# Spreading a per-batch softmax chain over the units of a spectral filter, its subtraction of one on another engine

## The chip, the cores and the metric

The kernel runs on one core of one Trainium2 chip. The metric is the time of one execution on the device in microseconds, the median of several runs.

## The reference

Three stages follow each other on `x` of 8 batches, 3072 tokens, 256 channels, all in float32.

```python
X = np.fft.rfft(x, axis=1)                       # per batch, along the tokens
y = np.fft.irfft(X * (filt_r + 1j * filt_i), n=3072, axis=1)
x = y.reshape(8 * 3072, 256)

logits = x @ phi                                 # 32 slots
d = np.exp(logits - logits.max(0, keepdims=True))     # softmax over ALL tokens
slot_input = (d / (d.sum(0, keepdims=True) + 1e-9)).T @ x
...                                              # 8 experts: relu(s @ w1[e]) @ w2[e]
c = np.exp(logits - logits.max(1, keepdims=True))     # softmax over the slots
x = (c / (c.sum(1, keepdims=True) + 1e-9)) @ slot_out

g, val = x @ w_gate, x @ w_val
out = (g / (1 + np.exp(-g)) * val) @ w_out
```

## The kernel before

`phase1` computes the filter, the logits and the first softmax; `transition` the experts; `phase2` the second softmax and the gated product. The change lies in `phase1` alone.

The FFT is two stages of matmuls. A **step** is one half (128 channels) of a batch, so there are 16 steps; a step has 6 **units**, so there are 96 units, numbered `i`, and 12 of them to a batch. One loop issues them, and since the schedule is manual, each engine's order is the order in which the Python code issues. In a unit stand, in this order:

- `s2_unit` (second stage): 8 matmuls into `X` (two PSUM buffers), which need the whole of `b`, the step's first-stage result; two products `P` and `Q` on VectorE; two sums on GpSimd into `y`.
- `tail_ops`: `tr_unit`, four transposes of the `y` of two units ago into `T` (one buffer) and a copy on ScalarE to `yt`; in every other unit `phi_pair`, the logits' matmuls into `L`, added up in `lts`. When a batch's last `lts` is there, its chain (below) is made and queued.
- `spread`: the ScalarE copies into `b` of the first-stage groups issued since.
- `aside`: one step of a side job (first the cutting of the weights from float64 to float32, `conv`, on VectorE, ScalarE and GpSimd; then `first_weights`, which reads logits back from memory).
- `pump(1)`: one step of the chain.
- `plan[u]`: which of the four first-stage groups of the **next** step (`s1_chunk`) this unit issues: a matmul group into `s` (one PSUM buffer), and its transposition on VectorE to `sg`, which `spread` copies in the next unit.
- a second `pump` in every third unit and in the last ten; a second `aside`.

The **chain** of a batch is a generator whose `yield`s cut it into steps: transposes of `lts` (L346), an inverse DFT (L356), transposes (L366) to `t4`, logits per token (L380) with their maximum `cm` on VectorE and a copy `lg` on ScalarE, an empty step, the maximum over the batch (L391), the subtraction of the maximum (L397, L400) and the exponential on ScalarE, minus one (L410; the constant part is put back at `dt`), a forward DFT (L415, `bd`, L422, `dt`, L443, `dh`), and the weighted sum of the filtered tokens (L453) into `sl`, which is stored. It runs during the next batch's units. The chains of batches 0 to 5 run in the full loop; that of batch 6 is stopped after 9 steps (`HOLD`) and finished with that of batch 7 after the loop, in an order written out by hand.

Where a chain step allocates `small()`, it takes the one PSUM buffer `c`; `lh`, `us`, `dt`, `dh` and `sl` take turns in one SBUF buffer each (tags `twa`, `twb`).

Of the kernel before, what the change touches and what calls it, by code (L numbers as in the profile page):

```python
# [17 lines left out]
NB, SEQ, D, E = 8, 3072, 256, 32  # L18
# [61 lines left out]
def spectral_softmoe_glu_kernel(  # L80
# [18 lines left out]
    pe, dve, act, pool = nc.tensor, nc.vector, nc.scalar, nc.gpsimd  # L99
# [32 lines left out]
    def phase1():  # L132
        with ExitStack() as c1:
# [30 lines left out]
            def load_x(step, k):  # L164
                b, h = divmod(step, 2)
                if b >= NB:
                    return

                if k == 0:
                    xt[step] = xp[step % 2].tile([128, 2, 16, 128], F32, tag="x", name="x")  # L170
                xr = x[b].rearrange("(p h r n) d -> r h p n d", h=2, r=2, n=16)
                for r in range(2):
                    nc.sync.dma_start(  # L173
                        out=xt[step][64 * r:64 * r + 48, k], in_=xr[r, k, :, :, h * 128:(h + 1) * 128]
                    )
# [91 lines left out]
            def tr_unit(step, u):  # L267
                b, h = divmod(step, 2)
                y = yt[b, u][:, :, :, h * 128:(h + 1) * 128]
                ps = ps_t.tile([128, 2, 2, 128], F32, tag="T", name="T")  # L270
                for i in range(2):
                    for ri in range(2):
                        pe.transpose(out=ps[:, i, ri, :], in_=y[:, i, ri, :], identity=ident)  # L273
                t = ytp.tile([128, 2, 2, 128], F32, tag="yt", name="yt")
                act.copy(t, ps)  # L275
                ytr[step, u] = t
# [24 lines left out]
            def chain(b, last):  # L301
# [3 lines left out]
                def two(late=False):  # L305

                    if late and b == NB - 2:
                        return [p.tile([128, 512], F32, tag=t, name="cl") for p, t in ((ps_t, "T"), (ps_l, "L"))]
                    if not last:
                        ps = small()  # L310
                        return [ps[:, 0:512], ps[:, 512:1024]]
                    banks[0] ^= 1
                    if not banks[0]:
                        return [ps_x.tile([128, 512], F32, tag="X", name="cl") for _ in range(2)]
                    ps = ps_s1.tile([128, 1024], F32, tag="s1", name="cl")
                    return [ps[:, 0:512], ps[:, 512:1024]]
# [18 lines left out]
                def col(t, k, n=128):  # L335

                    w = 512 // n
                    return t[k // w][:, k % w * n:(k % w + 1) * n]
# [4 lines left out]
                es2 = [slice(0, 16), slice(16, 32)]  # L343
# [10 lines left out]
                for jj in range(NJ):  # L354
                    g, k = jj % 4, jj // 4
# [16 lines left out]
                if last:  # L372
                    lg = [pq.tile([96, 16, 32], F32, tag="P", name="lg", bufs=3) for _ in es2]
                else:
                    lg = chp.tile([96, E, 32], F32, tag="lg", name="lg")
                    lg = [lg[:, es, :] for es in es2]
                cm = chp.tile([96, E], F32, tag="cm", name="cm")
                pl = two()
                for es, p in zip(es2, pl):
                    pe.matmul(out=p[0:96], lhsT=i2_sb, rhs=t4[:, es, :])  # L380
                for es, p, l in zip(es2, pl, lg):
                    dve.tensor_reduce(
                        out=cm[:, es], in_=p[0:96].rearrange("p (e n) -> p e n", n=32), axis=AX.X, op=ALU.max
                    )
                    act.copy(l, p[0:96].rearrange("p (e n) -> p e n", n=32))
                    nc.scalar.dma_start(out=lgd[b][:, es, :], in_=l)
                yield
# [10 lines left out]
                dd = chp.tile([96, E, 32], F32, tag="t4", name="dd")  # L398
# [6 lines left out]
                    )  # L405
                    act.activation(dd[:, es, :], dd[:, es, :], AF.Exp)
                if not last:
                    yield
                for es in es2:
                    (dve if last else pool).tensor_scalar_add(dd[:, es, :], dd[:, es, :], -1.0)  # L410
                yield
                bd = chp.tile([128, E, 32], F32, tag="lg", name="bd")
                pl = two()
# [6 lines left out]
                for jj in range(NJ):  # L420
                    g, k = jj % 4, jj // 4
# [28 lines left out]
                for q in range(3):  # L450
                    for ri in range(2):
                        for g in range(4):
                            pe.matmul(  # L453
                                out=ps[32 * g:32 * g + 32, 0:D],
                                lhsT=col(dh, 8 * q + 4 * ri + g, 32),
                                rhs=yt[b, 2 * q + g // 2][:, g % 2, ri, :],
                                start=(q == 0 and ri == 0),
                                stop=(q == 2 and ri == 1),
                                tile_position=(0, 32 * g),
                            )  # L460
                    if last and q:
                        rb, pss = next(com)
                    elif q == 1:
                        yield
                if b == NB - 2:
                    sl = slots[1][:, 2, :]
# [155 lines left out]
                spread()  # L622

            todo = []
            gens = []
            units = [(s, u) for s in range(2 * NB) for u in range(6)]
            plan = [[0], [1], [2], [3], [], []]

            steps = [0] * NB

            def pump(n):

                for _ in range(n):
                    while gens and steps[NB - 2] < HOLD:
                        b, g = gens[0]
                        steps[b] += 1
                        if next(g, 0) != 0:
                            break
                        gens.pop(0)

            def tail_ops(i):
                if 0 <= i - 2 < len(units):
                    tr_unit(*units[i - 2])
                if i - 4 >= 0 and i % 2 == 0 and i - 3 < len(units):
                    s, u = units[i - 4]
                    phi_pair(s, u // 2)
                    if s % 2 == 1 and u == 4:
                        gens.append((s // 2, chain(s // 2, s // 2 == NB - 1)))

            def aside():  # L650
                if next(side[0], 0) == 0 and len(side) > 1:
                    side.pop(0)

            for i, (s, u) in enumerate(units):
                if u in (0, 2):
                    load_x(s + 2, u // 2)
                s2_unit(s, u)
                tail_ops(i)
                spread()
                if i >= 4:  # L660
                    aside()
                pump(1)
                for c in plan[u]:
                    s1_chunk(s + 1, c)
                if u == 5:
                    bt.pop(s)
                pump(1 if i % 3 == 2 or i >= len(units) - 10 else 0)
                if i == 88:
                    kept(0)
                    kept(1)  # L670
                if i >= 4:
                    aside()
# [4 lines left out]
                flat_load(w1s[e], w1[e], 128)  # L677
            for i in range(len(units), len(units) + 4):
                tail_ops(i)
            (_, g6), (_, g7) = gens  # L680
            for g in (g7, g7, g7, g6, g7, g6, g7, g7, g6, g7, g6, g6):
                next(g, None)
            for _ in g7:
# [338 lines left out]
```

## Time and profile before

| | |
|---|---|
| median of 3 runs | 1586.67 us (1585.38 to 1588.87) |
| the profiled execution | 1588.74 us, of which the trace's span is 1587.0 us |
| mean granted TensorE clock | 0.977 of 2.4 GHz |
| TensorE busy (matmuls) | 1498.5 us, 94% |
| VectorE busy | 1186.1 us, 75% |
| ScalarE busy | 956.8 us, 60% |
| GpSimd busy | 257.9 us, 16%, nearly all of it in `phase1` |

The span is from the first to the last instruction. PE is TensorE's matmuls, PEld its weight loads, DVE VectorE, ACT ScalarE, POOL GpSimd. Times within the trace are in us from the span's start.

### The profile page before, as it was taken

Reading aid. Unit: us, or ns where it says so; the run is one execution under the profiler, and the core shown is the slowest. Engines: PE = TensorE matmul, PEld = TensorE weight load, DVE = VectorE, ACT = ScalarE, POOL = GpSimd, SP = SyncE. Lnnn points to the kernel's source line nnn. Section 1 sums busy time; section 2 is a strip of 40 time slices with the busy share of each in tenths; the row PEclk is TensorE's granted clock in tenths of the full one; section 3 lists DMA queues with packets and bytes.
Section 4 is the critical chain, followed back from the end, with each engine's and each line's share of the span. In section 5 each row is a group of like instructions: output and inputs, shape, how many; then the busy total and the mean of one; then the engine's idle time right before and its main releaser. Section 6 shows DMA issues by size and latency. Waiting matters only on the chain.

```text
span 1587.0 us, 26489 instructions
## 1 busy us (share of the span) xinstructions
PE 1498.5 (94%) x10218; PEld 1152.2 (73%) x10218; DVE 1186.1 (75%) x1946; ACT 956.8 (60%) x1808; POOL 257.9 (16%) x314
## 2 busy tenths in 40 slices
PE   4889998998886999999999999999999999999998
PEld 1455554554543888888888888888888888888887
DVE  1587777777633887797888788788878878977775
ACT  1364554554423766776676676667667667766665
POOL 0465655555401000000000000000000000000000
PEclk9899999999998999999999999999999999999999
DMA  9985758565767022102112111200211121121111
GB/s 175 175 142 102 128 101 150 112 110 89 263 201 196 14 54 50 27 23 59 37 27 58 33 27 34 70 19 23 67 37 27 41 51 28 32 49 28 27 28 27
DMA packets 105297, 116.58 MB, mean 73 GB/s; under 512 B 14770, under 2 KB 85172, under 8 KB 104916
## 3 DMA queue, kind: packets, MB, share of 16 engines
q1 hardware_dynamic: 102260, 110.44, 32.9%
q10 hardware_dynamic: 2656, 3.93, 1.0%
q8 instruction: 80, 1.31, 0.4%
q0 software_dynamic: 256, 0.52, 0.2%
q14 instruction: 45, 0.37, 0.1%
HBM read 68.21 MB, written 34.60 MB: 65 GB/s over the span
## 4 chain that ended last, share of the span: by engine, by line
PE 82%; DVE 7%; DMA 4%; SPq 2%; POOL 2%; issue 1%; ACT 1%; ACTq 0%; DVEq 0%; POOLq 0%
PE o L936 34%; PE o L940 17%; PE G L908 8%; PE V L909 8%; PE X L242 3%; PE s L211 3%; PE T L273 2%; DVE P L250 2%; DVE Q L251 1%; DVE sg L219 1%; POOL dd L410 1%; DMA c<-cd 1%; PE c L453 1%; DMA ft<-in_filt_i_dram 1%; SPq L173 1%
## 5 line engine op out<-in xcount | busy, mean ns | idle before, releaser
L936 PE MATMUL o<-wo,hi 128*128 128x512 f32 x2304 | 832.5, 395 | 0.0
L940 PE MATMUL o<-wo,lo 128*128 128x256 f32 x2304 | 645.1, 280 | 0.0
L911 ACT ACTIVATE s<-G 128x512 f32<-128x512 f32 x576 | 345.1, 599 | 326.5 <-PE G L908 323.6
L917 DVE TENSOR_TENSOR h<-V,s 128x512 f32<-128x512 f32 x576 | 394.8, 685 | 178.2 <-ACT s L911 177.2
L936 PEld LDWEIGHTS o<-wo,hi 128*128 128x128 f32 x2304 | 432.9, 188 | 103.8
L940 PEld LDWEIGHTS o<-wo,lo 128*128 128x128 f32 x2304 | 434.4, 189 | 25.5 <-DVE lo L925 0.4
L925 DVE TENSOR_TENSOR lo<-h,hi 128x512 fp32r<-128x512 f32 x576 | 417.0, 724 | 0.1
L924 ACT CAST hi<-h 128x512 fp32r<-128x512 f32 x576 | 354.7, 616 | 14.4 <-DVE h L917 10.2
L908 PE MATMUL G<-c,g 128*128 128x512 f32 x576 | 229.4, 398 | 9.3 <-DMA wo<-wod 5.0
L909 PE MATMUL V<-c,v 128*128 128x512 f32 x576 | 228.7, 397 | 1.3 <-DVE h L917 1.3
L242 PEld LDWEIGHTS X<-b,fwd 128*64 128x64 f32 x1536 | 88.5, 145 | 65.8 <-issue 47.9
L908 PEld LDWEIGHTS G<-c,g 128*128 128x128 f32 x576 | 108.8, 189 | 35.2 <-issue 10.5
L219 DVE STREAM_TRANSPOSE sg<-s 128x1024 f32<-128x1024 f32 x64 | 79.3, 1239 | 55.0 <-PE s L211 55.0
L211 PE MATMUL s<-x,csm 48*64 48x512 f32 x512 | 91.4, 724 | 29.6 <-DMA x<-in_x_dram 15.3
L242 PE MATMUL X<-b,fwd 128*64 128x128 f32 x1536 | 112.8, 292 | 4.3 <-ACT b L228 2.3
L275 ACT COPY yt<-T 128x512 f32<-128x512 f32 x96 | 56.1, 585 | 94.9 <-PE T L273 91.5
L855 POOL TENSOR_TENSOR lg<-lg,mx 96x1024 f32<-96x1024 f32 x7 | 16.8, 2405 | 592.7 <-DVE mx L853 592.7
L909 PEld LDWEIGHTS V<-c,v 128*128 128x128 f32 x576 | 109.3, 190 | 3.2 <-DVE h L917 2.4
L950 DVE TENSOR_TENSOR ot<-o,tmp 128x256 f32<-128x256 f32 x192 | 70.1, 422 | 38.8 <-ACT tmp L949 38.8
L263 POOL TENSOR_TENSOR y<-P 128x256 f32<-128x256 f32 x96 | 70.3, 732 | 153.3 <-DVE P L250 152.7
L228 ACT COPY b<-sg 128x768 f32<-128x768 f32 x64 | 58.3, 911 | 38.0 <-DVE sg L219 37.6
L250 DVE TENSOR_TENSOR P<-X,ft 128x512 f32<-128x512 f32 x96 | 65.2, 679 | 19.2 <-PE X L242 16.9
(195 smaller groups left out, 1056.3 us busy)
## 6 DMA issues: line engine op xcount, KB each, us to landing
x<-in_x_dram SPq DMA_DIRECT2D x64, 384.0 KB, 8.2
out_dram<-ot SPq DMA_DIRECT2D x192, 128.0 KB, 2.2
w<-in_moe_w_dram SPq DMA_DIRECT2D x16, 1024.0 KB, 9.8
c<-ch SPq DMA_DIRECT2D x42, 128.0 KB, 2.4
c<-cl SPq DMA_DIRECT2D x42, 128.0 KB, 2.4
raw<-in_moe_w_gate_dram SPq DMA_DIRECT2D x12, 256.0 KB, 5.0
lgd<-lg ACTq DMA_DIRECT2D x16, 192.0 KB, 5.3
raw<-in_moe_w_val_dram SPq DMA_DIRECT2D x12, 256.0 KB, 4.2
```

Of the source, the lines that this page charges most:

```text
L211: pe.matmul(out=ps[64 * k:64 * k + 64, 16 * r:16 * r + 16, :], lhsT=s1t_sb[64 * r:64 * r + 48, :], rhs=xt[step][64 * r:64 * r + 48, k, :, ...
L219: dve.transpose(out=sg.rearrange("p j d k -> p d j k"), in_=ps.rearrange("p n d -> p d n"))
L242: pe.matmul(out=ps[par * 64:(par + 1) * 64, i, ri, :], lhsT=fwd[:, j, ri * 64:(ri + 1) * 64], rhs=bb[:, j, :],)
L250: dve.tensor_tensor(out=P, in0=ps, in1=f, op=ALU.mult)
L908: pe.matmul(out=pg, lhsT=g4[c][:, fs], rhs=c4[b][:, q, G, :])
L909: pe.matmul(out=pv, lhsT=v4[c][:, fs], rhs=c4[b][:, q, G, :])
L911: act.activation(s, pg, AF.Silu)
L917: dve.tensor_tensor(out=h, in0=pv, in1=s, op=ALU.mult)
L924: act.copy(hi, h)
L925: dve.tensor_tensor(out=lo, in0=h, in1=hi, op=ALU.subtract)
L936: pe.matmul(out=a, lhsT=hi[:, ts], rhs=wo[f].rearrange("p k d -> p (k d)"), start=(f == 0), stop=(f == NF - 1), skip_group_check=True,)
L940: pe.matmul(out=a[:, D:2 * D], lhsT=lo[:, ts], rhs=wo[f][:, 0, :], start=False, stop=(f == NF - 1), skip_group_check=True,)
```

## The change

Four things. A finished batch's chain is queued only after the unit's first `pump`, so it starts one unit later. The chain gets one step a unit; the extra pump of every third unit goes, and the only step that is followed by another in the same unit is the one that ends in `yield "on"`, behind which the subtraction of one now stands: on VectorE for every batch, in the unit ahead of L415, which reads it. The weighted sum (L453) is cut in two for batch 6 only, and the two maxima are issued ahead of the two copies of `lg`. The first-stage groups move from units 0 to 3 of a step to units 1 to 4.

```diff
@@ chain
-                for es, p, l in zip(es2, pl, lg):
+                for es, p in zip(es2, pl):
                     dve.tensor_reduce(
                         out=cm[:, es], in_=p[0:96].rearrange("p (e n) -> p e n", n=32), axis=AX.X, op=ALU.max
                     )
+                for es, p, l in zip(es2, pl, lg):
                     act.copy(l, p[0:96].rearrange("p (e n) -> p e n", n=32))
                     nc.scalar.dma_start(out=lgd[b][:, es, :], in_=l)
...
                     act.activation(dd[:, es, :], dd[:, es, :], AF.Exp)
                 if not last:
-                    yield
+
+                    yield "on"
                 for es in es2:
-                    (dve if last else pool).tensor_scalar_add(dd[:, es, :], dd[:, es, :], -1.0)
+                    dve.tensor_scalar_add(dd[:, es, :], dd[:, es, :], -1.0)
                 yield
...
                     if last and q:
                         rb, pss = next(com)
-                    elif q == 1:
+                    elif q == 1 and b == NB - 2:
                         yield
@@ the loop
-            plan = [[0], [1], [2], [3], [], []]
+            plan = [[], [0], [1], [2], [3], []]
...
             def pump(n):
 
+                r = None
                 for _ in range(n):
                     while gens and steps[NB - 2] < HOLD:
                         b, g = gens[0]
                         steps[b] += 1
-                        if next(g, 0) != 0:
+                        r = next(g, 0)
+                        if r != 0:
                             break
                         gens.pop(0)
+                gens.extend(ready)
+                ready.clear()
+                return r == "on"
...
                     if s % 2 == 1 and u == 4:
-                        gens.append((s // 2, chain(s // 2, s // 2 == NB - 1)))
+                        ready.append((s // 2, chain(s // 2, s // 2 == NB - 1)))
...
-                pump(1)
+                on = pump(1)
                 for c in plan[u]:
                     s1_chunk(s + 1, c)
                 if u == 5:
                     bt.pop(s)
-                pump(1 if i % 3 == 2 or i >= len(units) - 10 else 0)
+                if on or i >= len(units) - 10:
+                    pump(1)
```

In the program the instructions of the lines behind the edits get other numbers: L391, L397, L400, L410, L415, L422, L443 and L453 become L392, L398, L401, L412, L417, L424, L445 and L455.

**First place**, TensorE around the reader of the subtraction, in a batch in the middle of the loop. Before, from the matmuls of the subtracted maximum on (L397, in unit 0 of the batch's second step):

```order
L397 MATMUL c<-dg,ones 96x32
L211 MATMUL s_2200<-x,csm 64x512 x4
L242 MATMUL X<-b,fwd 64x128 x8
L273 MATMUL T<-csm,y 128x128 x4
L211 MATMUL s_2239<-x,csm 64x512 x4
L242 MATMUL X<-b,fwd 64x128 x8
L273 MATMUL T<-csm,y 128x128 x4
L282 MATMUL L<-yt,phi_sb 32x256 x4
L415 MATMUL c<-dd,csm 128x512 x2
L211 MATMUL s_2289<-x,csm 64x512 x4
L422 MATMUL c<-fwd,bd 32x128 x24
```

After, the same stretch of the chain (now units 3 to 5):

```order
L398 MATMUL c<-dg,ones 96x32
L211 MATMUL s_2310<-x,csm 64x512 x4
L242 MATMUL X<-b,fwd 64x128 x8
L273 MATMUL T<-csm,y 128x128 x4
L282 MATMUL L<-yt,phi_sb 32x256 x4
L417 MATMUL c<-dd,csm 128x512 x2
L211 MATMUL s_2360<-x,csm 64x512 x4
L242 MATMUL X<-b,fwd 64x128 x8
L273 MATMUL T<-csm,y 128x128 x4
L424 MATMUL c<-fwd,bd 32x128 x24
```

The reader L415 (now L417) stood two units behind L397 and stands one unit behind it now; the DFT that follows (L422, now L424) has a second-stage group and transposes ahead of it that it had not.

**Second place**, VectorE in the same stretch. Before:

```order
L400 TENSOR_TENSOR dd<-lg,c 96x512 x2
L219 STREAM_TRANSPOSE sg<-s_2200 128x32x16x2
L556 TENSOR_SCALAR ex<-raw 128x256
L557 TENSOR_SCALAR mn<-raw 128x256
L250 TENSOR_TENSOR P<-X,ft 128x512
L251 TENSOR_TENSOR Q<-X,ft 128x512
L219 STREAM_TRANSPOSE sg<-s_2239 128x32x16x2
```

After:

```order
L393 TENSOR_REDUCE mb<-c 32x1
L395 TENSOR_SCALAR dg<-csm,mb 32x32
L219 STREAM_TRANSPOSE sg<-s_2267 128x32x16x2
L558 TENSOR_SCALAR ex<-raw 128x256
L559 TENSOR_SCALAR mn<-raw 128x256
L250 TENSOR_TENSOR P<-X,ft 128x512
L251 TENSOR_TENSOR Q<-X,ft 128x512
L401 TENSOR_TENSOR dd<-lg,c 96x512 x2
L219 STREAM_TRANSPOSE sg<-s_2310 128x32x16x2
L412 TENSOR_SCALAR dd<-dd 96x512 x2
L565 SCALAR_TENSOR_TENSOR ex<-raw,ex 128x256
```

The two subtractions of one (L412) are new on this engine; ahead of them stands the transposition of the unit's first-stage group.

**Third place**, TensorE around the border of two steps, from the last first-stage group on (the fourth one of four). Before:

```order
L211 MATMUL s_2065<-x,csm 64x512 x4
L242 MATMUL X<-b,fwd 64x128 x8
L273 MATMUL T<-csm,y 128x128 x4
L282 MATMUL L<-yt,phi_sb 32x256 x4
L380 MATMUL c<-t_2062,csm 96x512 x2
L242 MATMUL X<-b,fwd 64x128 x8
L273 MATMUL T<-csm,y 128x128 x4
L391 MATMUL c<-csm,cm 32x96
L242 MATMUL X<-b,fwd 64x128 x8
```

After:

```order
L211 MATMUL s_2091<-x,csm 64x512 x4
L242 MATMUL X<-b,fwd 64x128 x8
L273 MATMUL T<-csm,y 128x128 x4
L366 MATMUL c<-csm,usa 128x128 x4
L366 MATMUL c<-csm,usb 128x128 x2
L242 MATMUL X<-b,fwd 64x128 x8
```

The last row of both is the first second-stage group of the next step, which reads what the first row's group becomes; two units stood between them, now one does.

## Rows read from the trace of the kernel before

**Rows 1.** The page: busy share by engine; granted clock in 40 slices.
```profile
PE 1498.5 (94%) x10218; PEld 1152.2 (73%) x10218; DVE 1186.1 (75%) x1946; ACT 956.8 (60%) x1808; POOL 257.9 (16%) x314
...
PEclk9899999999998999999999999999999999999999
```

**Rows 2.** Loop periods of 12 units: busy us by engine (count), clock, DMA share, GB/s.
```profile
196.34:247.60 51.26, 46.81 (x529) 26.75 (x532) 38.45 (x66) 26.97 (x56) 29.19 (x39) 0.93 0.71 119
...
350.16:401.40 51.24, 45.70 (x522) 26.25 (x523) 40.08 (x62) 23.62 (x45) 27.33 (x34) 0.93 0.59 108
```

**Rows 3.** TensorE over one period in order of time: start, us, instructions [idle before].
```profile
208.89 0.26 PE L391 MATMUL c<-csm,cm 96*32 96x96 f32 x1 [1.12 <-ACT lg L385]
...
215.00 1.09 PE L211 MATMUL s<-x,csm 48*64 48x512 f32 x8 [0.76 <-DVE sg L219]
...
219.46 1.13 PE L415 MATMUL c<-dd,csm 96*128 96x512 f32 x2 [1.19 <-POOL dd L410]
220.91 1.73 PE L415 MATMUL c<-dd,csm 96*128 96x512 f32 x2 [0.33 <-POOL dd L410]
222.57 1.99 PE L211 MATMUL s<-x,csm 48*64 48x512 f32 x8
224.49 2.80 PE L422 MATMUL c<-fwd,bd 128*32 128x128 f32 x48
...
247.16 0.44 PE L346 MATMUL c<-csm,lts 128*128 128x128 f32 x2 [1.05 <-DVE lts L296]
```

**Rows 4.** Stretches of 0.8 us behind L415; columns as in Rows 2.
```profile
221.60:222.40 0.80, 0.80 (x2) 0.00 (x0) 0.00 (x0) 0.00 (x0) 0.80 (x2) 0.50 1.19 127
...
228.00:228.80 0.80, 0.80 (x13) 0.63 (x10) 0.30 (x2) 0.65 (x3) 0.00 (x0) 0.92 0.00 0
```

**Rows 5.** VectorE, ScalarE, GpSimd in order of time ahead of L415, same period.
```profile
212.52 1.26 DVE L400 TENSOR_TENSOR dd<-lg,c 96x512 f32<-96x512 f32 x2
...
213.22 1.23 ACT L406 ACTIVATE dd<-dd 96x512 f32<-96x512 f32 x2 [1.45 <-DVE dd L400]
...
217.46 3.40 POOL L410 TENSOR_SCALAR dd<-dd 96x512 f32<-96x512 f32 x2
```

**Rows 6.** Line 410 over the trace: count, duration in ns (least, median, most).
```profile
L410 POOL TENSOR_SCALAR dd<-dd x14: 1481/1492/1952, 114.9 to 418.8; 96x512 f32<-96x512 f32 x14
...
L410 DVE TENSOR_SCALAR dd<-dd x2: 422/423/424, 447.5 to 448.1; 96x512 f32<-96x512 f32 x2
```

**Rows 7.** Line 556 in the same form.
```profile
L556 DVE TENSOR_SCALAR ex<-raw x36: 239/300/828, 65.4 to 352.4; 128x256 int32<-128x256 int32 x36
```

**Rows 8.** TensorE in order of time: a unit without a first-stage group, and the next.
```profile
198.73 1.09 PE L242 MATMUL X<-b,fwd 128*64 128x128 f32 x16
...
201.00 1.09 PE L211 MATMUL s<-x,csm 48*64 48x512 f32 x8
```

**Rows 9.** Groups of the period from 196.34: busy us, mean ns of one | idle before.
```profile
L219 DVE STREAM_TRANSPOSE sg<-s 128x1024 f32<-128x1024 f32 x8 | 9.9, 1240 | 3.4 <-PE s L211 3.4
...
L250 DVE TENSOR_TENSOR P<-X,ft 128x512 f32<-128x512 f32 x12 | 8.2, 681 | 2.0 <-PE X L242 1.9
...
L228 ACT COPY b<-sg 128x768 f32<-128x768 f32 x8 | 7.3, 915 | 0.1
L275 ACT COPY yt<-T 128x512 f32<-128x512 f32 x12 | 7.0, 584 | 9.6 <-PE T L273 9.1 <-PE c L391 0.4
```

**Rows 10.** TensorE in the last loop period: its longest wait.
```profile
371.67 1.98 PE L211 MATMUL s<-x,csm 48*64 48x512 f32 x8 [3.61 <-DVE sg L219]
```

**Rows 11.** Waits in that period (us in total, times, longest).
```profile
DVE mx L582 <- DMA lgf<-lgd: 2.6, 1, 2.6
```

**Rows 12.** TensorE in the last twelve units, the chain of batch 6.
```profile
413.24 0.26 PE L391 MATMUL c<-csm,cm 96*32 96x96 f32 x1 [0.55 <-ACT lg L385]
...
418.87 1.12 PE L415 MATMUL c<-dd,csm 96*128 96x512 f32 x2 [1.30 <-POOL dd L410]
```

**Rows 13.** The store of `sl`, line 471: us from issue to landing.
```profile
DMA to landing us min/median/max: 6.0/7.5/7.9
```

More of the change, by code (lines that the diff above doesn't have):

```diff
@@ L624, in phase1 @@
             todo = []
-            gens = []
+            gens, ready = [], []
             units = [(s, u) for s in range(2 * NB) for u in range(6)]
-            plan = [[0], [1], [2], [3], [], []]
+            plan = [[], [0], [1], [2], [3], []]
             steps = [0] * NB
             def pump(n):
+                r = None
                 for _ in range(n):
@@ L679, in phase1 @@
                 tail_ops(i)
-            (_, g6), (_, g7) = gens
+            (_, g6), (_, g7) = gens + ready
             for g in (g7, g7, g7, g6, g7, g6, g7, g7, g6, g7, g6, g6):
```

## The prediction

> **What bounds the kernel now.** The page first: over the whole span TensorE is busy 94% and the granted clock is near full, but in the first twelve of the 40 slices, which are `phase1`, the clock line shows 8s and 9s [rows 1]. So I read `phase1` period by period. From 94 to 401 us the trace repeats itself: six periods of 12 units (one batch's filter and the chain of the batch before), all of some 51.2 us, the sixth with something else in it. The reader is to see in the row of one of the first five that TensorE is busy 46.81 of 51.26 us, that its mean clock is 0.93, and that VectorE, the next busiest, is at 38.45, 75% [rows 2]. TensorE sets the pace, with 4.45 us of idle time and a slow spell in it.
>
> The idle time is read in order of time [rows 3]. It has four places: L346 waits 1.05 us for the addition of the last logits to `lts`, issued in the same unit; L391 waits 1.12 for the copy of `lg`; a first-stage group waits 0.76 for the transposition ahead of it; L415 waits 1.19 and 0.33 for the two subtractions of one on GpSimd. The sum is 4.45, all of the idle time of the period. Behind L415 the same work takes twice as long: the eight matmuls of a first-stage group 1.99 us instead of 1.09. The stretches of 0.8 us say why: the granted clock is 0.50, that is 1.2 of 2.4 GHz, at 221.6 and back at 0.92 by 228.0 [rows 4]. About 7 us at half speed cost 3.5, which a mean clock of 0.93 over 51.26 us gives too. Without idle time and slow spell the period would be 51.26 - 4.45 - 3.5 = 43.3 us.
>
> Why L415 waits: VectorE has subtracted the maximum at 213.8, ScalarE has done the exponentials at 214.5, and only at 217.46 does GpSimd begin, which issues the subtraction a unit later and behind two sums and a piece of the weights' cutting; it takes 3.40 us for the two [rows 5].
>
> **The change part by part.**
>
> *The chain starts a unit later.* L346 then finds `lts` long done: -1.05 us a period. Its `lts` buffer is written by the next batch a unit after L346, so nothing new waits.
>
> *One step a unit, maxima ahead of the copies.* L392 (was L391) stands two units behind its logits, with the empty step between: -1.12. The first-stage group that waited 0.76 stood behind the subtraction of the maximum (two instructions, 1.26 us) on VectorE; that group has another neighbour now: -0.76, though the other may wait (below). The pieces behind L417 have a unit between each other.
>
> *The subtraction on VectorE.* GpSimd loses 3.40 us, which nobody will miss, VectorE gains two instructions. Their price: the same operation on VectorE, in the last batch's chain, takes 0.42 us each [rows 6]. Is it there in time? From the start of its unit TensorE needs 1.0 + 0.6 (second-stage group and transposes), 0.3 (L398, two short matmuls, an estimate), 1.0 (first-stage group), then in the next unit 1.0 + 0.6 + 0.6 until it wants L417: 5.1 us. VectorE in this time: `P` and `Q` from 1.0 on (0.68 each, 1.2 for both as they overlap), the two subtractions of the maximum 1.26 [rows 5], the transposition 1.24 [rows 9], and 0.42 for the first half. That ends at 5.1 if VectorE has no backlog, so a wait of 0. With a backlog as long as one unit's maximum, diagonal and cutting, which stand ahead (some 1.2 us), it ends at 6.3: a wait of 1.2. Before, VectorE was behind at such a place (the 0.76 us), so I take 1.1; the ends stay for the range. The second half comes while L417 works on the first.
>
> That price has a second end. L556, a short VectorE instruction with one operand from SBUF, takes 0.24 us at least but 0.83 at most [rows 7], the long ones beside running GpSimd sums. Two subtractions could so cost 1.9 us in place of 0.85. The Trainium skill (page "SBUF — State Buffer", section "Who interferes with whom") says that such an instruction of VectorE can take a port pair that it shares with GpSimd, and that whoever issues second is blocked for the other's whole instruction; that speaks against moving work from GpSimd to VectorE while GpSimd goes on. By it the wait at L417 would be up to 2.2 us, by the row of the last chain 1.1. I stay with 1.1, since GpSimd has only the unit's two sums there and is done with them while VectorE is still at the transposition.
>
> *First-stage groups in units 1 to 4.* This removes a distance. The last group of a step is now copied to `b` in unit 5, behind that unit's `yt` copy, and the next unit's second-stage group needs it. TensorE in unit 5, in a step with L366: 198.73 to 201.00, so 2.27 us [rows 8]. ScalarE meanwhile: the `yt` copy waits for the transposes (1.6 us into the unit), takes 0.58, then the copy to `b` 0.92 [rows 9]: 3.1 us, with the hand-overs 3.15. So TensorE waits 0.9 at this border. In the other step of the batch, unit 5 has L424, 1.4 us at full clock (half of L422's 2.80 at half clock, [rows 3]) in place of 0.7: the wait is 0.2. New: +1.1 a period. The lower bound is 0 (if TensorE is late anyway), the upper 2 x 2.1, if VectorE's transposition is 1.2 late as well.
>
> *Small things.* `sl` ends two units nearer to the next `lh`, which takes its buffer: copy 0.4, issue 0.35, landing 7.5 [rows 13] are 8.2 us, against some 8 us until ScalarE gets there, and 2 more until L356 wants it. I price it at 0. The hand-overs in new places I price at 0.5 us a period, an estimate.
>
> **The sum.** The slow spell followed 1.5 us of waiting at L415 close behind 0.76, and not the 1.12 at L391 nor the 1.05 at L346. With single waits of 0.9 and 1.1 left, I take the clock to stay at full: -3.5. A period: -4.45 - 3.5 + 1.1 (L417) + 1.1 (borders) + 0.5 = -5.25, so 46.0 us. Five periods: -26.2. The sixth has another wait: a first-stage group stands 3.61 us [rows 10], since VectorE waits 2.6 for logits read back [rows 11]; its total is 5.54 idle and 3.5 of slow clock. VectorE keeps that wait, but in the units that follow it no first-stage group is issued at first, so I let TensorE keep 2.6 of it beside the 2.7 above: -9.0 + 5.3 = -3.7. In the last twelve units L391 and L415 waited 0.55 and 1.30 [rows 12]; there the extra pump puts L398 right behind L392, with two short VectorE instructions between: some 1.1, as L391 waited for a copy, and 0.3 at L417. Net -0.5. Start-up: the first wait on the weights' load stays where it is. Together -26.2 - 3.7 - 0.5 = -30.4. The transition begins with what `phase1` releases, its loads too, so it moves along as a whole.
>
> The profiled execution took 1588.74 us, 2.1 above the median: 1588.7 - 30.4 = 1558.3 like it, and **1556** as a median.
>
> **The rivals.**
>
> (a) *The clock still falls once a period.* L417 waits 1.9 us (backlog and GpSimd's sums), and the rest is as above. Then a period is 46.0 + 0.8 + 3.5 = 50.3, a gain of 1.0: with the sixth and the end some 7 us, 1580. For it: VectorE is fullest just there. Against: the second wait right behind (0.33) is gone. The port rule of the Trainium skill's page "SBUF — State Buffer", cited above, would lead here.
>
> (b) *The subtraction is in time and nothing else is lost.* The period is 46.0 - 1.1 - 0.5 = 44.4, a gain of 6.9: 5 x 6.9 + 5.3 + 0.8 = 41, so 1546; without the border waits too 43.3, and 1540. For it: VectorE's sum without backlog gives just this.
>
> (c) *Slower: the borders.* If the last group's transposition comes 1.2 us late at both borders, behind `bd` and the subtractions, TensorE waits 2.1 at each and falls to half clock behind each: 2 x (2.1 + 3.5) + 1.1 = 12.3 against 7.95 removed, +4.4 a period, 1586.7 + 26 = 1613. It decides from 6.9 us of border costs a period on, that is one slow spell and 1.7 us of waiting at each. Against: at the second border TensorE has 1.4 us of L424 to do, and VectorE itself has only 75% to do.
>
> (d) *No change: VectorE takes over.* Its busy time rises to 39.3 us; if what TensorE no longer waits for at L415 it waits for at `X` and `s`, the period stays near 51.3: 1586. Against: that needs 12 us of idle VectorE in every period.
>
> **The numbers.** Chances: my sum 0.57, (b) 0.18, (a) 0.14, (c) 0.06, (d) 0.05. The own range of my sum is 1548 to 1566 (the wait at L417 between 0 and 2.2 at full clock, the sixth period between the others' gain and none). The whole range reaches into (b) and (a): 1542 to 1579. A change of 0.2%, 3 us, is about what can be told here; faster takes the first three but a twentieth, 0.88; the same 0.06; slower 0.06.
>
> **What would show it.** Right: periods of 45 to 47 us with the clock at 1.00, no wait at L346 and L392, a wait of about 0.9 before the first second-stage group of every other step with the copy to `b` as its releaser, and one of about 1 at L417, released by VectorE. Wrong: 0.50 of clock anywhere between 100 and 380 us; new waits at `X` or `s` of more than 1 us a period; VectorE's two subtractions at over 0.6 us each.

## The result and the profile after

The changed kernel takes 1564.43 us in the median of 4 runs (1558.03 to 1567.84), the kernel before, run beside it, 1586.03 (1580.75 to 1588.87): ratio 0.9873, interval 0.9845 to 0.9901. A second set of 5 runs gave 0.9873 again (0.9850 to 0.9896). That is 20 us faster, 16 to 25 by the interval, where 30 were forecast; the range held it. The profiled execution, at 1558.03 us with a span of 1556.2, is the fastest of its four.

The trace cut into periods, each from the first matmul of L346 of one chain to that of the next (busy us by engine, then granted clock, DMA share, GB/s; [rows 2] before):

```profile
91.77:137.42 45.65, 43.09 (x527) 25.54 (x526) 37.76 (x71) 26.80 (x56) 26.86 (x38) 1.00 0.81 140
137.42:183.05 45.63, 43.09 (x528) 25.55 (x526) 37.40 (x70) 26.84 (x56) 26.30 (x37) 1.00 0.79 138
183.05:229.03 45.98, 43.26 (x527) 25.44 (x526) 37.55 (x70) 26.75 (x56) 26.45 (x37) 1.00 0.73 131
229.03:274.64 45.61, 43.09 (x527) 25.55 (x526) 37.41 (x70) 26.81 (x56) 26.29 (x37) 1.00 0.80 137
274.64:320.64 46.00, 43.09 (x527) 25.55 (x526) 37.41 (x70) 26.82 (x56) 26.29 (x37) 1.00 0.76 130
320.64:375.73 55.09, 49.36 (x507) 27.71 (x506) 39.80 (x64) 23.88 (x45) 24.27 (x31) 0.85 0.53 81
```

Five periods are as the sum had them (46.0), at full clock, with TensorE busy 43.1 of 45.6 us. The sixth is not: 55.1 us, clock 0.85, TensorE busy 49.4 us with fewer matmuls. TensorE in order of time, the waits of the second period and then of the sixth ([rows 3] and [rows 10] before):

```profile
146.85 1.09 PE L242 MATMUL X<-b,fwd 128*64 128x128 f32 x16 [0.81 <-ACT b L228]
...
155.08 0.63 PE L273 MATMUL T<-csm,y 128*128 128x128 f32 x4 [0.44 <-ACT yt L275]
...
156.21 0.26 PE L392 MATMUL c<-csm,cm 96*32 96x96 f32 x1
...
163.75 1.96 PE L417 MATMUL c<-dd,csm 96*128 96x512 f32 x4 [1.17 <-DVE dd L412]
...
183.05 0.82 PE L346 MATMUL c<-csm,lts 128*128 128x128 f32 x6
...
341.67 1.99 PE L211 MATMUL s<-x,csm 48*64 48x512 f32 x8 [0.98 <-DVE sg L219]
...
354.73 3.57 PE L417 MATMUL c<-dd,csm 96*128 96x512 f32 x4 [2.37 <-DVE dd L412]
```

No wait is left at L346 and L392; three small ones are there, 2.4 us together. What holds L417 up is VectorE, in the same period:

```profile
159.02 0.53 DVE L558 TENSOR_SCALAR ex<-raw 128x256 int32<-128x256 int32 x1
159.47 0.28 DVE L559 TENSOR_SCALAR mn<-raw 128x256 int32<-128x256 int32 x1
159.68 0.68 DVE L250 TENSOR_TENSOR P<-X,ft 128x512 f32<-128x512 f32 x1
...
160.87 1.27 DVE L401 TENSOR_TENSOR dd<-lg,c 96x512 f32<-96x512 f32 x2
162.07 1.23 DVE L219 STREAM_TRANSPOSE sg<-s 128x1024 f32<-128x1024 f32 x1
163.23 0.71 DVE L412 TENSOR_SCALAR dd<-dd 96x512 f32<-96x512 f32 x2
```

It stands idle nowhere between these rows. It begins `P` at 159.68, 1.2 us after that `X` was done (at 158.5), and the transposition lies between the subtraction of the maximum and that of one.

In the sixth period the wait at L417 is twice as long, and the eight matmuls of a first-stage group at 341.67 take 1.99 us, L417 itself 3.57 instead of 1.96: half clock (0.50 from 342 to 350 and from 356 to 360 us). VectorE in that period waits for the logits that are read back ([rows 11] before):

```profile
332.86 1.00 DVE L584 TENSOR_REDUCE mx<-lgf 96x16 f32<-96x512 f32 x1 [2.16 <-DMA lgf<-lgd]
...
350.90 1.01 DVE L584 TENSOR_REDUCE mx<-lgf 96x16 f32<-96x512 f32 x1 [3.94 <-DMA lgf<-lgd]
351.84 1.27 DVE L401 TENSOR_TENSOR dd<-lg,c 96x512 f32<-96x512 f32 x2
...
354.20 0.71 DVE L412 TENSOR_SCALAR dd<-dd 96x512 f32<-96x512 f32 x2
```

Before, VectorE waited for one of the two reads of the first batch's logits. Now it waits for both, and the second wait stands right ahead of the two instructions for which L417 waits. The first of the two slow spells begins ahead of that second wait, behind 1.44 us at L273 (at 339.30, for a `yt` copy) and the 0.98 us of the row at 341.67.

The time by stretches, in us from the span's start, read off the first L346 of a chain and the first sum of an output tile on VectorE in `phase2`:

| kernel | chain 0 | chain 5 | chain 6 | chain 7 | first output | span |
|---|---|---|---|---|---|---|
| before | 91.99 | 348.01 | 401.12 | 434.83 | 531.12 | 1587.0 |
| before, second trace | 93.53 | 346.75 | 399.71 | 433.41 | 529.45 | 1585.3 |
| after | 91.77 | 320.64 | 375.73 | 409.33 | 500.39 | 1556.2 |
| after, second trace | 94.05 | 323.35 | 379.91 | 414.11 | 507.36 | 1563.1 |

Between the first traces: start -0.2, five periods -27.1 (256.0 to 228.9), sixth +2.0 (53.1 to 55.1), last twelve units -0.1, from there to the first output -5.2, and the rest, 1055.9 and 1055.8, the same. The second trace of the changed kernel has the five periods the same (229.3), the sixth at 56.6, the last twelve units at 34.2, and 2.3 and 2.2 us more at the start and in the transition. The sixth period before is 53.1 us here and 51.24 in [rows 2]: the window there begins 2.15 us later, behind L346 and its wait, and ends only 0.28 us later.

### The profile page after: what moved, and what is told of

It reads as the page before. It is cut to its first block, busy times and chain, and to the rows that moved or that the text cites. A ratio compares the mean times of both kernels' runs of the same rounds, so it can differ in the third digit from the quotient of the medians.

```text
span 1556.2 us, 26502 instructions
## 1 busy us (share of the span) xinstructions
PE 1477.5 (95%) x10218; PEld 1146.6 (74%) x10218; DVE 1182.4 (76%) x1960; ACT 954.1 (61%) x1808; POOL 238.3 (15%) x300
## 4 chain that ended last, share of the span: by engine, by line
PE 84%; DVE 4%; DMA 4%; SPq 3%; ACT 2%; issue 2%; POOL 0%; ACTq 0%; DVEq 0%; POOLq 0%
PE o L944 34%; PE o L948 17%; PE V L917 9%; PE G L916 9%; PE X L242 4%; PE T L273 3%; PE s L211 2%; DMA c<-cd 1%; PE c L455 1%; SPq L173 1%; SPq L129 1%; PE L L282 1%; PE c L417 1%; DMA raw<-in_moe_w_gate_dram 1%; DVE sg L219 1%
## 5 line engine op out<-in xcount | busy, mean ns | idle before, releaser
L242 PEld LDWEIGHTS X<-b,fwd 128*64 128x64 f32 x1536 | 86.9, 143 | 76.7 <-issue 51.7
L211 PE MATMUL s<-x,csm 48*64 48x512 f32 x512 | 84.7, 679 | 22.0 <-DMA x<-in_x_dram 15.2
L251 DVE TENSOR_TENSOR Q<-X,ft 128x512 f32<-128x512 f32 x96 | 64.9, 677 | 13.7 <-POOL y L263 13.7
## 6 DMA issues: line engine op xcount, KB each, us to landing
raw<-in_moe_w_gate_dram SPq DMA_DIRECT2D x12, 256.0 KB, 4.5
raw<-in_moe_w_val_dram SPq DMA_DIRECT2D x12, 256.0 KB, 3.5
```

What stands on the lines that cost most here:

```text
L211: pe.matmul(out=ps[64 * k:64 * k + 64, 16 * r:16 * r + 16, :], lhsT=s1t_sb[64 * r:64 * r + 48, :], rhs=xt[step][64 * r:64 * r + 48, k, :, ...
L242: pe.matmul(out=ps[par * 64:(par + 1) * 64, i, ri, :], lhsT=fwd[:, j, ri * 64:(ri + 1) * 64], rhs=bb[:, j, :],)
```

## The experiments

The theory is that the waits and the slow clock behind L415 were the cost, that the subtraction's engine takes both away, that the other moves trade waits of about 1 us, and that the sixth period has a matter of its own. The rival is that the new spacing and the groups' new units carry the gain.

### The changed kernel again

> The changed kernel once more, for a tighter ratio and a second trace. The first trace has five loop periods of 45.6 to 46.0 us instead of 51.3 (predicted 46.0), but a sixth of 55.1 instead of 51.2, in which VectorE waits 2.2 and 3.9 us for logits read back from memory and the clock falls. Theory A: the five periods are the same in every execution (45.6 to 46.0), and what differs between runs (1558 to 1568) lies in the sixth period and in the transition's loads. Rival B: the clock falls in some of the five periods in other executions, so that one of them is near 49 here. A ratio of 0.985 to 0.989.

Median 1564.51 us, ratio 0.9873 (0.9850 to 0.9896). Its five periods are 45.65, 45.65, 46.02, 45.76 and 46.22 us, all at a clock of 1.00; the sixth is 56.56. This is Theory A: the clock does not fall in the five.

### One word: the subtraction on VectorE, nothing else

```diff
 # in the kernel before
-                    (dve if last else pool).tensor_scalar_add(dd[:, es, :], dd[:, es, :], -1.0)
+                    dve.tensor_scalar_add(dd[:, es, :], dd[:, es, :], -1.0)
```

> The kernel before with one word changed: the subtraction of one on VectorE, in its old place in the order. Theory A (the wait at L415 and the slow clock behind it were what mattered, and the new places give back most of what they save): L415 no longer waits, the clock stays at full, the period falls from 51.3 to 51.3 - 1.5 - 3.5 = 46.3 us, that is within 1 us of the changed kernel's; total 1586 - 25 = 1561, ratio 0.984. Rival B (the chain's new spacing and the groups' new units carry the gain): VectorE is late too, L415 still waits over 1 us, the clock still falls, period 49 to 51, ratio 0.99 to 1.0.

Median 1564.73 us, ratio 0.9878 (0.9857 to 0.9900): no different from the whole change as far as these intervals tell. One of its periods, by engine:

```profile
138.44:185.48 47.04, 43.40 (x529) 25.39 (x525) 39.67 (x69) 27.10 (x57) 26.08 (x36) 1.00 0.72 128
```

and TensorE's waits in the next:

```profile
200.17 0.26 PE L391 MATMUL c<-csm,cm 96*32 96x96 f32 x1 [1.12 <-ACT lg L385]
206.28 1.09 PE L211 MATMUL s<-x,csm 48*64 48x512 f32 x8 [0.76 <-DVE sg L219]
...
209.48 1.98 PE L415 MATMUL c<-dd,csm 96*128 96x512 f32 x4
...
213.18 1.55 PE L422 MATMUL c<-fwd,bd 128*32 128x128 f32 x48 [0.70 <-DVE bd L341]
...
234.21 0.44 PE L346 MATMUL c<-csm,lts 128*128 128x128 f32 x2 [1.05 <-DVE lts L296]
```

L415 does not wait, the clock is full, and the three other waits of the kernel before are all still there, with one of 0.7 at L422. The period is 47.0, as Theory A had it, with 0.7 us more than its 46.3. The five periods are 234.8 us (91.77 to 326.56), 5.9 and 5.5 more than in the two traces of the whole change. Of what the whole change wins by that, it gives most back in the sixth period (55.1 and 56.6 against 54.0) and in the last twelve units (33.6 and 34.2 against 32.0); the 1 to 3 us that are left can't be told in the ratios.

The price of the subtraction on VectorE, in ns (least, median, most), in the place of the kernel before, and then in that of the changed kernel ([rows 6] before):

```profile
L410 DVE TENSOR_SCALAR dd<-dd x16: 411/574/950, 113.7 to 425.9; 96x512 f32<-96x512 f32 x16
```

```profile
L412 DVE TENSOR_SCALAR dd<-dd x16: 372/403/424, 117.6 to 422.5; 96x512 f32<-96x512 f32 x16
```

In the new place no GpSimd instruction runs beside the two in the six batches of the loop, and the price is 0.40 us. In the old place two sums of GpSimd run beside them (113.30 to 114.03 and 113.99 to 114.90, the two subtractions 113.74 to 115.18), and it goes up to 0.95. That agrees with the rule of the Trainium skill's page "SBUF — State Buffer" ("Who interferes with whom") that, of two instructions of VectorE and GpSimd that need the port pair they share, the one that issues second is blocked. It bears on the old place and not on the new.

### The first-stage groups back in units 0 to 3

```diff
 # in the changed kernel
-            plan = [[], [0], [1], [2], [3], []]
+            plan = [[0], [1], [2], [3], [], []]
```

> The changed kernel with the first-stage groups back in units 0 to 3. Theory A: the wait of 0.8 us for the last copy to b before the first second-stage group of every other step goes, and the wait at L417 stays near 1.2: period 44.9, ratio 0.985 against before at the changed kernel's 0.987, so 4 us less than the changed kernel. Rival B: the groups stand in the same units as the logits and their two maxima then, the waits at s and L417 grow by more than 0.8, and the period is 46.5 or more, so no better than the changed kernel.

Median 1560.01 us, ratio 0.9852 (0.9827 to 0.9877); the changed kernel, run beside it, 1564.51. The wait for `b` is gone, that at L417 grows from 1.2 to 1.5, and the second to fourth periods are 44.5 (143.22 to 187.68) and 44.8. So moving the groups costs some 1.2 us in such a period, as Theory A had it. The first and fifth, with other waits, are 46.6 and 45.2, and the five together 3.3 us shorter than in the changed kernel; the intervals of the two ratios overlap.

### More time for the read-back

```diff
 # in the changed kernel, first_weights
                     nc.sync.dma_start(out=lg, in_=lgd[0][:, :, 16 * G:16 * G + 16])
                     yield
+                    yield
+                    yield
                     mx = chp.tile([96, 1, 16], F32, tag="mx0", name="mx0")
```

> The changed kernel with two more steps between the reading back of the first batch's logits and the maximum that VectorE takes of them, so one unit more for the transfer. Theory A: VectorE's two waits (2.2 and 3.9 us) shrink to under 1 us, the wait of 2.4 at L417 and the slow clock of the sixth period go, and that period falls from 55 to 47 or 48: 7 us less than the changed kernel, ratio 0.983. Rival B: the sixth period is long because of the work of the first weights on VectorE, not the wait; it stays at 52 or more, gain under 3 us.

Median 1554.99 us, ratio 0.9811 (0.9785 to 0.9837), 9.5 us below the changed kernel, run beside it. The sixth period:

```profile
321.53:367.63 46.10, 41.65 (x508) 24.18 (x506) 39.11 (x64) 24.22 (x45) 23.78 (x30) 1.00 0.58 83
```

VectorE no longer waits for the reads, the clock stays at 1.00, and 55 us become 46.1, with the same work on VectorE, as Theory A had it. TensorE is busy 41.65 us instead of 49.36 with the same matmuls, and idle 4.3 instead of 5.6: of the 9.0 us, 7.7 are the slow clock and 1.3 the waits themselves.

### The changed kernel with the subtraction on GpSimd

```diff
 # in the changed kernel
-                    dve.tensor_scalar_add(dd[:, es, :], dd[:, es, :], -1.0)
+                    (dve if last else pool).tensor_scalar_add(dd[:, es, :], dd[:, es, :], -1.0)
```

> The changed kernel with the subtraction of one back on GpSimd (but for the last batch), in its new place. Theory A (its engine decides): from the end of the exponentials GpSimd needs 1.5 us for each half where VectorE needs 0.42, so the wait at L417 grows from 1.2 to 2 or 3 us in two pieces, the clock falls again once a period, and the period goes from 45.7 to 50 or 51: total about 1588, ratio 0.995 to 1.005. Rival B (the new order is enough, since the exponentials end when VectorE would begin, and GpSimd has less to do there): a wait of under 2 us, full clock, period 46.5, ratio 0.99.

Median 1578.74 us of 12 runs (1567.93 to 1581.37), ratio 0.9964 (0.9944 to 0.9985). Two neighbouring periods, and TensorE at L417 in the second:

```profile
141.32:187.70 46.38, 43.38 (x527) 25.45 (x526) 36.77 (x68) 26.86 (x56) 29.24 (x39) 1.00 0.71 134
187.70:237.20 49.50, 46.51 (x528) 26.78 (x527) 37.00 (x68) 26.82 (x56) 29.23 (x39) 0.93 0.64 118
```

```profile
214.15 1.12 PE L417 MATMUL c<-dd,csm 96*128 96x512 f32 x2 [1.30 <-POOL dd L412]
215.61 2.08 PE L417 MATMUL c<-dd,csm 96*128 96x512 f32 x2 [0.33 <-POOL dd L412]
```

Neither expectation came true as a whole. The waits are only 1.30 (once 1.42) and 0.33 in every period, as the rival had it, but the clock falls behind them in two of five periods (49.5 us) and not in three (46.4 to 46.6). The median is 14 us above that of the changed kernel. In the traces some 3 come from the waits themselves (0.7 a period), 6 from the two slow spells, and 5 from the last twelve units, 39.0 us (385.64 to 424.68) instead of 33.6, where L417 waits 2.87 and the clock falls again; differences at the start, in the sixth period and in the transition go both ways.

### The copies to b first

```diff
 # in the changed kernel, the loop
                 s2_unit(s, u)
-                tail_ops(i)
                 spread()
+                tail_ops(i)
```

> The changed kernel with the copies to b ahead of the unit's yt copy on ScalarE. Theory A: the wait of 0.8 us before the first second-stage group of every other step goes, nothing else grows, and the period falls from 45.7 to 44.9: 4 to 5 us in all against the changed kernel, ratio 0.984. Rival B: yt is late instead (the transposes wait for it already, 0.4 us a period), or VectorE, not reached by this wait any more, lets L417 wait 0.8 longer: no gain, ratio 0.987.

Median 1559.29 us, ratio 0.9836 (0.9814 to 0.9858). A period is 44.8 us (137.98 to 182.81), the wait for `b` is gone, and the one at L417 is 1.34 in four of five, which it was in two of the ten periods of the changed kernel (1.17 to 1.19 in the others). This is Theory A, though the first period does not gain (45.8): the five take 225.7 us against 228.9 and 229.3. In the sixth period, with its reads, L417 waits 5.4 instead of 2.4, and it takes 56.3 us.

### The empty step behind the subtraction

```diff
 # in the changed kernel, chain
                 yield
-                if not last:
-                    yield
                 ps = small()
                 pe.transpose(out=ps[0:32, 0:96], in_=cm, identity=ident[0:96, 0:96])
...
                     dve.tensor_scalar_add(dd[:, es, :], dd[:, es, :], -1.0)
                 yield
+                if not last:
+                    yield
```

> The changed kernel with the empty step of the chain moved from ahead of the maximum (L392) to behind the subtraction of one, so that the maximum comes a unit sooner and L417 stands two units behind L398. Theory A: the wait of 1.2 us at L417 goes, and one of about 1 us comes at L392, for the copies of lg that empty its buffer; a period of 45.5, as before within 0.5, but in the sixth period the 2.4 at L417 goes: total 0 to 4 us less. Rival B: L392 finds all done, and the period falls by the whole 1.2 to 44.5: 8 us less, ratio 0.982.

Median 1562.84 us, ratio 0.9851 (0.9826 to 0.9875). L417 waits no more; the maximum, one unit sooner, does (its line is 390 here):

```profile
151.49 0.26 PE L390 MATMUL c<-csm,cm 96*32 96x96 f32 x1 [1.42 <-ACT lg L386]
```

The period stays at 45.7 (134.89 to 180.59). The wait has only changed its place, as Theory A had it. In the fourth period the clock falls behind that wait (0.96, 46.9 us), in the four others it does not.

### More time for the read-back, in the kernel before

The same two `yield`s in the kernel before.

> The kernel before with the same one unit more between the reading back of the first logits and the maximum of them. Theory A (the long sixth period is a matter of its own, only made worse by the change): its wait of 3.6 us at the first-stage group goes, but the subtraction on GpSimd stays, so the sixth period becomes like the others, 51.3, or a little longer: 0 to 3 us less than before, where the changed kernel won 9 by the same edit. Rival B: it wins as much here, 7 us or more, ratio 0.995.

Median 1585.40 us of 12 runs, ratio 0.9994 (0.9971 to 1.0017). The wait of 3.6 us is gone, and L415 waits 1.83 instead, with the clock at half behind it. The sixth period falls by 1.4 us (53.1 to 51.7), but the last twelve units rise by 3.4 (33.7 to 37.1), with 1.96 us of waiting at L346. From L346 of chain 5 to the first output it is 184.8 us, against 183.1 and 182.7 in the two traces of the kernel before. Theory A holds for the total: the edit that wins 9.5 behind the change wins nothing that can be told ahead of it.

### The kernel before again

> The kernel before once more, for a second trace. In two other kernels with the subtraction on GpSimd the waits at its reader were the same in every period (1.2 or 1.3 and 0.33 us), but the clock fell to half behind some of them and not behind others. Theory A: so it does in the kernel before; its first trace, with about 7 us at half clock in every period, is one end. A second execution has the same waits, a period of 48.6 us where the clock stays and up to 51.3 where it falls, and its time is lower the fewer slow periods it has: 1588.7 less up to 2.7 us for each. Rival B: in this kernel the slow spell is there in every period of every execution: 51.2 to 51.3 again in all five.

1587.05 us, one run. TensorE behind L415 in the second period, and L415 in the third and fourth:

```profile
171.09 1.13 PE L415 MATMUL c<-dd,csm 96*128 96x512 f32 x2 [0.33 <-POOL dd L410]
173.62 1.55 PE L422 MATMUL c<-fwd,bd 128*32 128x128 f32 x48 [0.39 <-DVE bd L341]
...
219.67 1.49 PE L415 MATMUL c<-dd,csm 96*128 96x512 f32 x2 [0.33 <-POOL dd L410]
...
270.94 1.55 PE L415 MATMUL c<-dd,csm 96*128 96x512 f32 x2 [0.33 <-POOL dd L410]
```

The waits (1.2 and 0.33) are the same in all; in the second period L415 and L422 run at full speed (L422 1.55 us, 2.80 in [rows 3]) and the period is 48.6 us (144.36 to 192.95), in the third and fourth the half clock has begun within L415 and they are 51.3. This is Theory A. In the first period too the clock does not fall behind L415; there it is at half for some 3 us from 97.7 on, behind a wait of 1.68 us at L346.

### Both edits that helped

> The changed kernel with both edits that helped: the logits read back one unit earlier than they are needed, and the copies to b ahead of yt. Theory A (the two waits are apart from each other): 9.5 and 5 us add up, about 1550, ratio 0.978; periods of 44.8, the sixth near 46. Rival B: the copies to b ahead of yt make the wait at L417 in the sixth period longer (5.4 us there against 2.4), so that they do not add up: 1555, ratio 0.981.

Median 1551.79 us of 6 runs, ratio 0.9806 (0.9774 to 0.9837). In the trace both waits are gone: the six periods take 270.2 us (94.34 to 364.51) against 284.0 in the changed kernel and 276.1 with the read-back alone, and the sixth is 45.2, as Theory A had it. In the ratios it can't be told: 0.9774 would be the sum, which the interval just reaches, and 0.9811 is the read-back alone.

### And the subtraction ahead of the transposition

```diff
 # in addition, the loop
                 on = pump(1)
+                if on:
+                    pump(1)
                 for c in plan[u]:
                     s1_chunk(s + 1, c)
                 if u == 5:
                     bt.pop(s)
-                if on or i >= len(units) - 10:
+                if i >= len(units) - 10:
                     pump(1)
```

> The same with the subtraction of one ahead of the unit's first-stage group and of its transposition on VectorE. Theory A (the transposition, 1.2 us, is what makes L417 wait 1.3): VectorE waits a little for the exponentials instead, and the wait at L417 falls to about 0.4; the period falls to 44.0, 4 to 5 us in all: 1545, ratio 0.975. Rival B: ScalarE's exponentials end no earlier than VectorE gets to the subtraction now, so VectorE stands idle for them and the transposition and everything behind it comes as much later: L417 waits 0.8 or more, gain under 2 us, ratio 0.977.

Median 1552.57 us, ratio 0.9808 (0.9775 to 0.9842): no gain. TensorE's waits:

```profile
162.11 1.95 PE L417 MATMUL c<-dd,csm 96*128 96x512 f32 x4 [0.39 <-DVE dd L412]
168.95 1.09 PE L242 MATMUL X<-b,fwd 128*64 128x128 f32 x16 [0.56 <-ACT b L228]
171.65 0.66 PE L445 MATMUL c<-csm,dta 128*128 128x128 f32 x4 [0.45 <-ACT dtb L437]
```

L417 waits 0.4, as Theory A had it, but 1.0 us comes back behind it, at the border and at L445, and the period is 45.2 (137.32 to 182.53), 0.4 more than without. So the total goes as Rival B had it, though at other places than it named; that the transposition, which now comes behind the subtraction, is what makes these two late was not tested.

### The read-back and the groups back

The two `yield`s of the read-back and the first `plan`, in the changed kernel.

> The changed kernel with the logits read back earlier and the first-stage groups back in units 0 to 3. Theory A: with the groups back a period was 44.5 with a wait of 1.5 at L417; the sixth period loses its long wait (4.7 us at L417) and the slow clock: 1560 - 9.5 = 1550, ratio 0.978, the same as with the groups moved and the copies to b first, so moving the groups brings nothing of its own. Rival B: the read's wait meets the groups in units 5 and 0, so less is won: 1555.

Median 1553.54 us, ratio 0.9813 (0.9778 to 0.9847). The second to fourth periods are 44.5, the fifth 45.9 and the sixth 46.5: in these two the clock falls (0.96 and 0.93), in the fifth behind a single wait of 1.47 us at L417, which it does not behind 1.47 and 1.48 in the others. So the slow clock of the sixth is not gone, against Theory A. The total can't be told from the kernel with the groups moved and the copies to `b` first, as Theory A had it.

## Why the prediction was right, and where it was too large

**Right, and by its own steps.** The period after (46.0 forecast, 45.6 to 46.2 in ten periods of two traces), the wait at L417 (1.1; 1.17 to 1.34 measured) with VectorE's backlog of 1.2 us as its reason, no wait at L346 and L392, and the wait at the border (0.9; 0.81 measured; the second one, 0.2, is not there) came as forecast. The five periods: -26.2 forecast, -27.1 and -26.7 measured against the first trace of the kernel before. The choice between the two prices of the subtraction (0.42, and the upper end by GpSimd's sums) went the right way, as the 403 ns show.

The 0.5 us of new hand-overs has the right size (0.44 us for a `yt` copy) by luck. That wait is no hand-over: on ScalarE the `yt` copy stands behind both copies of `lg`, and these now begin only when both maxima are done:

```profile
152.38 0.58 ACT L386 COPY lg<-c 96x512 f32<-96x512 f32 x1 [2.85 <-DVE cm L382]
...
154.35 0.58 ACT L275 COPY yt<-T 128x512 f32<-128x512 f32 x1 [0.38 <-ACT lg L386]
```

In the last twelve units -0.5 was forecast and -0.1 measured: L417 waits 1.20 there, where I had 0.3.

**The sixth period.** Forecast was -3.7, measured +2.0 and +3.5. The step that failed is the slow clock: the "-9.0" takes its 3.5 us out of the sixth period too ("I take the clock to stay at full"), although 2.6 us of the read's wait are kept there. TensorE's idle time came out near the sum, 5.6 and 6.0 us for the 5.3 forecast, but the clock fell for longer than before, and TensorE is busy 49.4 us where the same matmuls take 41.65 at full clock: 7.7 us. A clock of 0.50 between 100 and 380 us is one of the signs of being wrong that the prediction names; for this period it came.

Why it falls goes back to the reads. "VectorE keeps that wait" followed the first one only. There are two, 18 us apart; the second had not made VectorE wait before. In the kernel before, 6.2 us lay between its issue (379.02) and the maximum (385.21), with VectorE at the transposition of `bd` and other work; with the chain in its new place VectorE comes to the maximum 0.2 us after the issue (346.77) and waits 3.9 us, right ahead of L401 and L412. The experiment that takes both waits away keeps the clock at full and wins 9.5 us, and the same edit in the kernel before none, so this is a cost of the change.

**The slow clock.** The step "-3.5" a period was read off one trace in which the clock fell in every period. In the second trace of the kernel before it does not fall behind L415 in two of the five periods, nor does it always in other kernels with the same waits. Where it stays at full, the period is 48.6 us, so 2.7 less and not 3.5: TensorE is busy 3.1 us less, and L422 then waits 0.39 for `bd`. The five periods of that second trace are 2.8 us shorter. That the median of the kernel before holds fewer slow spells than the trace on which the sum was made is likely, but two traces don't show it. The step "I take the clock to stay at full" held in all ten periods; it needed some luck, since in two variants the clock fell once behind a single wait of 1.42 and of 1.47 us.

**The sum.** 30.4 forecast, 20 measured: 6 to 7 us are the sixth period and about 3 the slow clock of the five, if the median is like the second trace; what is left is within the interval. That the first trace came out at 1558.0, where 1558.3 was forecast for it, is chance: the sixth period's miss is offset there by 5.2 us in the transition, which I had as 0. There TensorE waits for loads, and the stretch from chain 7 to the first output is anywhere between 90.8 and 96.6 us in the traces of this study; why was not followed.

**What carries the gain.** The engine of the subtraction, alone, gives as much as the whole (0.9878 against 0.9873), and the new order with the subtraction left on GpSimd gives 0.9964. Within a period the new spacing is worth 2.2 to 2.6 us on top of the engine (47.0 to 44.5 and 44.8, the groups in their old units), and moving the groups takes some 1.2 of it back. What is left, 5.5 to 5.9 us in five periods, is mostly given back in the sixth and in the last twelve units.

## What to carry to other kernels

When the releaser of the worst wait is one operation on a slow engine, try the operation on another engine in its old place first: here one word gave what the whole rearrangement gave. Before a schedule is shifted, list every transfer that an in-order engine waits for and see which work comes to stand behind it; a wait that cost nothing may be put ahead of the critical operation. A cost that comes from the clock is to be read from more than one execution before it goes into a sum.

## What was not expected of the hardware

The clock's fall to half behind the same waits is not the same in every period: behind 1.2 and 0.33 us it fell in the kernel before in five of five periods in one execution and in three of five in another. Behind a wait of 1.17 to 1.34 us in one piece it did not fall in the first five periods of the changed kernel's two traces. Behind one of 1.4 to 1.5 it did in single periods: in the fourth with the empty step moved (1.42) and in the fifth with the read-back and the groups back (1.47), and not in their neighbours with the same wait. What tells them apart these records don't show.

Issuing a store from ScalarE's queue holds ScalarE up. Most of the 16 issues of L387 take 0.31 us. In the second trace of the changed kernel one takes 0.87, and the `yt` copy behind it makes TensorE wait 1.00 instead of 0.44:

```profile
293.71 0.87 ACTq L387 DMA_DIRECT2D lgd<-lg  x1
294.62 0.58 ACT L275 COPY yt<-T 128x512 f32<-128x512 f32 x1 [0.94 <-PE X L242]
...
295.35 0.63 PE L273 MATMUL T<-csm,y 128*128 128x128 f32 x4 [1.00 <-ACT yt L275]
```
